# Halves of a partition's rows outermost in the tiles of q, k and v

## The chip, the cores and the metric

The kernel runs on one core of one Trainium2 chip. A core has five engines with queues of their own: PE (TensorE, matmuls, with PEld as the loading of its weights), DVE (VectorE), ACT (ScalarE), POOL (GpSimd) and SP (SyncE, which issues transfers here). Sixteen DMA engines move data. The metric is device microseconds of an execution, as a median over runs.

## The reference

Four batches, eight heads, 768 rows, head size 64, eight blocks of 96 rows. A Sinkhorn matrix P (8x8 for each head) mixes the blocks of k and of v; each block of q then attends to the mixed block at its own place; the result goes through a token-mixing layer.

```python
for _ in range(5):
    P = P - np.max(P, axis=-1, keepdims=True)
    P = np.exp(P)
    P = P / (np.sum(P, axis=-1, keepdims=True) + 1e-09)
    P = P / (np.sum(P, axis=-2, keepdims=True) + 1e-09)
k_sorted = np.einsum('bhij,bhjcd->bhicd', P, k_b).reshape(B, H, S, D)
v_sorted = np.einsum('bhij,bhjcd->bhicd', P, v_b).reshape(B, H, S, D)
scores = scale * np.matmul(q_b, k_sb.transpose(0, 1, 2, 4, 3))
...
attn_out = np.matmul(attn, v_sb).reshape(B, H, S, D)
...
wq, wk = x @ w_q, x @ w_k
W_tok = scale * np.einsum('bsd,btd->bst', wq, wk)
mixed = np.einsum('bst,btd->bsd', W_tok, x)
out = np.maximum(mixed, 0.0) @ w_out
```

## The kernel before

A batch's q, k or v (8 heads x 768 rows x 64, in f32) is loaded by one transfer that casts to bf16. Row 6p + r of a head lies in partition p at place r, so 128 partitions hold 6 rows of each head; a block of 96 rows is 16 partitions. The tiles Qn, Kn and Vn (three buffers each, NIN) are [128, head, 6 rows, 64]. `u_l` (L238 to L241) issues a load on POOL's queue: n = 0, 1, 2 is q, k, v. In DRAM a run of 6 rows of one head is contiguous, so a load is 128 x 8 pieces of 384 elements.

The work is cut into small units, each a letter with a batch, a number and an engine or a bank of PSUM. The list `ORDER` at the top of the file is their order, written out by hand; a unit is issued on its engine when the list comes to it, and waits there by semaphores for the data it reads and the buffers it writes. Each engine runs its own units in that order and never overtakes. `l` loads, `n` builds M (the Sinkhorn weights spread to a 128x128 matrix for each head; L231 to L236, on POOL or DVE), `Q` transposes q with the identity (L255), `K` sorts and transposes k with M (L264 to L277), `S` computes scores, `e` their exponential, `P` the attention output, `x` divides by the row sums; `T`, `J`, `W`, `G`, `H` and `O` are the layer behind, `y` the stores. Lower-case letters are mostly the copies out of PSUM. All matmuls go through the helper `mm` (L148), all copies through `copy` (L151), so the profile shows them as L149, L153 and L155 and they are told apart by their tiles.

v takes two ways. For batches 0 and 1 (`TURN`) it is sorted and transposed like k and then turned back by transposes (`F`). For batches 2 and 3 `V` (L282 to L289) sorts without a transpose: for each pair of rows n (2n and 2n + 1) eight matmuls with M as weights and 128 columns of Vn (two rows of a head) as the moving side; `v` (L291) copies the pair of all heads into Vs, and `R` (L298) moves one row of Vs to VT with a transfer on SP's queue.

The first entries of ORDER for POOL are the loads of k, v and q of batch 0, then q of batch 1, and further loads between the products for M. The queue works them off in the order k0, v0, q0, q1, k1, v1, k2, q2, the two halves of wqk, v2, q3, k3, v3, wo. Ahead of the sorting, TensorE runs 40 matmuls of zeros (`Z`) while the Sinkhorn steps run on DVE and ACT. At the end of the program stands a test of the row sums and a slower way behind an `If`, which these inputs don't take; the diff touches its loads too.

Of the kernel before, what the change touches and what calls it, by code (L numbers as in the profile page):

```python
# [56 lines left out]
def kernel(  # L57
# [11 lines left out]
    nc = tc.nc  # L69
    B, H, S, D = q.shape  # L70
# [3 lines left out]
    P = 128  # L74
    R6 = S // P
    SP = BLK // R6
    NP = H // 2
    D1 = D + 1
    DM = moe_w_out.shape[0]
# [18 lines left out]
    def tiles(name, n, shape, dtype=BF16):  # L98
        return [sb.tile(shape, dtype, name=f"{name}{i}") for i in range(n)]

    PS = psp.tile([P, 8, 512], FP32, name="ps")
    ENG = {"A": nc.scalar, "D": nc.vector, "P": nc.gpsimd, "S": nc.sync}
# [2 lines left out]
    nc.sync.dma_start(out=Pm[:, 0:NB, :], in_=sort_net.rearrange("b h i j -> (b h) i j"))  # L105

    NIN = 3
    Qn, Kn, Vn = (tiles(n, NIN, [P, H, R6, D]) for n in ("Qn", "Kn", "Vn"))
    wqk = sb.tile([P, PT, 2, DH], BF16, name="wqk")
    wo = sb.tile([P, PT, DM], BF16, name="wo")  # L110
    QT = tiles("QT", 2, [P, NP, R6, P])
# [1 line left out]
    Vs = tiles("Vs", 2, [P, R6, H, D1])  # L113
    VT = tiles("VT", 2, [BLK, NB, H * D1])
# [9 lines left out]
    ot = tiles("ot", NOT, [P, 2, DM], FP32)  # L124
    M = tiles("M", 2, [P, H, SP, NB])
    RS = sb.tile([BLK, B, NG, 2, AG // 2], FP32, name="RS")
# [3 lines left out]
    PbT = sb.tile([BH, 2, BH], BF16, name="PbT")  # L130
    Lx = sb.tile([BH, 4, NB, SP], BF16, name="Lx")
    tmp = sb.tile([BH, NB], FP32, name="tmp")
    idb = sb.tile([P, P], BF16, name="idb")
# [14 lines left out]
    def mm(o, w, x, start=True, stop=True, t=False):  # L148
        nc.tensor.matmul(o, w, x, is_transpose=t, start=start, stop=stop, skip_group_check=True)  # L149

    def copy(e, o, i):  # L151
        if e == "A":
            nc.scalar.copy(o, i)  # L153
        else:
            nc.vector.tensor_copy(o, i)  # L155

    def bf(n):
        return PS[:, n, :].bitcast(BF16)
# [76 lines left out]
            in1=m_p.unsqueeze(1).unsqueeze(3).to_broadcast([P, 2, SP, NB]), op=ALU.mult)  # L235


    def u_l(b, n, e):  # L238
        t, src = (Qn, Kn, Vn)[n], (q, k, v)[n]
        nc.gpsimd.dma_start(out=t[b % NIN].rearrange("p h r d -> p h (r d)"),  # L240
                            in_=src[b].rearrange("h (p r) d -> p h (r d)", p=P))  # L241

    def u_m(b, n, e):
        if n < 2:
# [10 lines left out]
    def u_Q(b, n, bank):  # L255
        ps = bf(bank)[:, 0:S].rearrange("p (r s) -> p r s", r=R6)
        for r in range(R6):
            for hh in range(2):
                mm(ps[hh * D:(hh + 1) * D, r, :], Qn[b % NIN][:, 2 * n + hh, r, :], idb, t=True)

    def u_q(b, n, e, bank):
        copy(e, QT[b % 2][:, n].rearrange("p r s -> p (r s)"), bf(bank)[:, 0:S])
# [1 line left out]
    def sorted_t(t, b, n, bank):  # L264
        ps = flat(bank)
        for r in range(R6):
            for hh in range(2):
                h = 2 * n + hh
                mm(ps[hh * D:(hh + 1) * D, r * P:(r + 1) * P], t[b % NIN][:, h, r, :],
                   M[b % 2][:, h].rearrange("p s i -> p (s i)"))  # L270

    def by_block(e, o, bank):
# [9 lines left out]
    def u_V(b, n, bank):  # L282
        if b in TURN:
            sorted_t(Vn, b, n, bank)
            return
        ps = flat(bank)
        for h in range(H):
            mm(ps[:, h * P:(h + 1) * P], M[b % 2][:, h].rearrange("p s i -> p (s i)"),
               Vn[b % NIN][:, h, 2 * n:2 * n + 2, :].rearrange("p r d -> p (r d)"))  # L289

    def u_v(b, n, e, bank):  # L291
        if b in TURN:
            by_block(e, XT[b % 2][:, n, :], bank)
            return
        copy(e, Vs[b % 2][:, 2 * n:2 * n + 2, :, 0:D].rearrange("p r h d -> p h r d"),
             flat(bank).rearrange("p (h r d) -> p h r d", h=H, r=2))

    def u_R(b, n, e):  # L298
        ENG[e].dma_start(out=VT[b % 2].rearrange("(s r) i x -> r s i x", r=R6)[n],
                         in_=Vs[b % 2][:, n].rearrange("p h e -> p (h e)"))  # L300

    def u_F(b, n, bank):
        for i in range(NB):
# [7 lines left out]
    def u_N(b, n, e):  # L311
        t = dict(q=QT, k=KT, v=Vs, f=VT, e=E, x=X)[e][b % 2]
        if e == "q":
            src = t[0:1, n, R6 - 1, P - 1:P]
        elif e == "k":
            src = t[0:1, n, S - 1:S]
        elif e == "v":
            src = t[0:1, 2 * n + 1, H - 1, D - 1:D]
        elif e == "f":
            src = t[0:1, NB - 1, (2 * n + 1) * D1:(2 * n + 1) * D1 + 1]  # L320
        elif e == "e":
            src = t[0:1, n, 0:1]
        else:
            src = t.rearrange("p k i m -> p (k i m)")[0:1, grp(n)[0] * D:grp(n)[0] * D + 1]
        nc.gpsimd.tensor_copy(gate, src)
# [125 lines left out]
    for item in ORDER.split():  # L451
        kind, b, n, arg = UNIT.match(item).groups()
        b, half = int(b), halves.get(n[-1], ())
# [22 lines left out]
    with tc.If(redo > 0, preferred_fallthrough_block=False):  # L476
        qc = QT[1].rearrange("p k r s -> p k (r s)")
        sx = XT[1][0:BLK].rearrange("p t c -> p (t c)").bitcast(FP32)[:, 0:S]
        ex = E[1][:, 1, 0:S]
        exT = E[1][:, 2, 0:S]  # L480
        mx = RS.rearrange("p b n a t -> p (b n a t)")[:, 0:NB]
        sm = RS.rearrange("p b n a t -> p (b n a t)")[:, NB:2 * NB]

        def bb(t, w):
            return t.unsqueeze(2).to_broadcast([BLK, NB, w])

        spread(0, H, BH)
        u_u(0, 1, "D", 0)
        for b in range(B):
            for n in range(3):  # L490
                nc.gpsimd.dma_start(out=(Qn, Kn, Vn)[n][0].rearrange("p h r d -> p h (r d)"),
                                    in_=(q, k, v)[n][b].rearrange("h (p r) d -> p h (r d)", p=P))
            if b == 0:
                spread(1, 0, H)
                src = PS[:, 1, 0:NB * H].rearrange("p (i h) -> p h i", h=H)
            else:
                src = PTR.rearrange("p i h -> p h i")[:, (b - 1) * H:b * H, :]
            for n in range(NP):
                spread_m("D", 0, n, src)
            for n in range(NP):  # L500
                u_Q(0, n, 2)
                u_q(0, n, "D", 2)
                copy("D", qc[:, n].rearrange("p (i r s) -> p r i s", i=NB, r=R6),
                     QT[0][:, n].rearrange("p r (i s) -> p r i s", i=NB))
                u_K(0, n, 4)
                u_k(0, n, "D", 4)
                sorted_t(Vn, 0, n, 6)
                by_block("D", XT[0][:, n, :], 6)
                u_F(0, n, 3)
                u_f(0, n, "D", 3)  # L510
            for h in range(H):
                kp, o = h // 2, h % 2 * D
                sp = PS[0:BLK, 4:6, 0:4 * BLK].rearrange("p a (i c) -> p a i c", c=BLK)
                for i in range(NB):
                    mm(sp[:, i // 4, i % 4, :], qc[o:o + D, kp, i * BLK:(i + 1) * BLK],
                       KT[0][o:o + D, kp, i * BLK:(i + 1) * BLK])
                copy("D", sx.rearrange("p (a n) -> p a n", a=2), PS[0:BLK, 4:6, 0:4 * BLK])
                s3 = sx.rearrange("p (i c) -> p i c", i=NB)
                nc.vector.reduce_max(mx, s3, axis=AX.X)
                nc.vector.tensor_sub(s3, s3, bb(mx, BLK))  # L520
                nc.scalar.activation(ex, sx, ACT.Exp, scale=scale)
                nc.vector.reduce_sum(sm, ex.rearrange("p (i c) -> p i c", i=NB), axis=AX.X)
                nc.vector.reciprocal(sm, sm)
                for i in range(NB):
                    mm(bf(6)[0:BLK, i * BLK:(i + 1) * BLK], ex[:, i * BLK:(i + 1) * BLK],
                       idb[0:BLK, 0:BLK], t=True)
                copy("D", exT, bf(6)[0:BLK, 0:S])
                op = PS[0:BLK, 7, :].rearrange("p (i d) -> p i d", d=D)
                for i in range(NB):
                    mm(op[:, i, :], exT[:, i * BLK:(i + 1) * BLK], VT[0][:, i, h * D1:h * D1 + D])  # L530
                nc.vector.tensor_mul(X[0][:, kp, :, o:o + D], op, bb(sm, D))
            for n in range(PT):
                u_T(0, n, n % 2)
                u_t(0, n, "D", n % 2)
            for n in range(2):
                u_J(0, n, 2)
                u_j(0, n, "D", 2)
                u_d(0, n, "D")
                u_W(0, n, 3)
                u_w(0, n, "D", 3)  # L540
            for n in range(2):
                u_G(0, n, 2)
            u_g(0, 0, "D", 2)
            for n in range(3):
                u_H(0, n, 4)
                u_h(0, n, "D", 4)
            for n in range(R6):
                u_O(0, n, n % 2)
                u_o(b, n, "D", n % 2)
                if b == LAST or n % 2:  # L550
                    u_y(b, n if b == LAST else n // 2, "P")
# [30 lines left out]
```

## Time and profile before

| | us |
|---|---|
| median of 3 runs | 108.27 (107.89 to 108.35) |
| the profiled execution, its own time | 108.6 |
| its span, first to last instruction | 106.8 |
| TensorE busy | 94.2 (88%) |
| DVE busy | 74.1 (69%) |
| ACT busy | 69.9 (65%) |
| POOL busy | 31.3 (29%) |

| transfer, by the page's part 6 | times | KB each | median us, issue to landing |
|---|---|---|---|
| Kn from k | 4 | 768 | 12.8 |
| Vn from v | 4 | 768 | 14.7 |
| Qn from q | 4 | 768 | 15.1 |
| wo | 1 | 512 | 22.7 |
| wqk, each of two | 1 | 64 | 14.3, 14.7 |
| VT from Vs | 12 | 130 | 2.5 |

The KB are those written. A busy share is over the whole span; the span has stages with different limits, and the page's rows of 40 slices (2.67 us each) show where. "Landing" counts from the issue, so it holds the time that a load stands in the queue behind others. Granted TensorE clock: 0.981 in the mean; it falls only in the last slices, where TensorE has no work.

### The profile page before, as it was taken

How to read it: one execution, taken by the hardware profiler on the slowest of the kernel's cores; microseconds unless marked ns; L12 is line 12 of the kernel's file. 1: busy time of each engine (PE TensorE's matmuls, PEld its weight loads, DVE VectorE, ACT ScalarE, POOL GpSimd, SP SyncE). 2: the span in 40 equal slices, each digit the busy share in tenths (PEclk: the TensorE clock that was granted, in tenths of full speed). 3: DMA queues.
4: the chain of work that ended last, by engine and by line, in shares of the span. 5: the costliest groups of instructions: out<-in, count | busy, mean ns of one | idle time of the engine just before them, and what ended most of it. 6: DMA issues, size and time to landing. Idle time of an engine off the chain costs nothing.

```text
span 106.8 us, 3637 instructions
## 1 busy us (share of the span) xinstructions
PE 94.2 (88%) x1556; PEld 65.7 (61%) x1556; DVE 74.1 (69%) x144; ACT 69.9 (65%) x101; POOL 31.3 (29%) x51
## 2 busy tenths in 40 slices
PE   5999989597698979889999999999999999999600
PEld 2334489486686966779868867597666565454300
DVE  2687689198797785788989977999767765455200
ACT  4101079769687879898879798688933448784400
POOL 5999089999229400000000000000077000000000
PEclk9999999999999999999999999999999999999975
DMA  0899999999999999999975373100059145496950
GB/s 3 91 201 205 203 203 210 200 203 205 205 204 204 188 202 211 198 203 208 205 161 159 94 211 96 44 6 0 6 196 388 45 196 203 160 408 236 381 196 18
DMA packets 18501, 18.57 MB, mean 174 GB/s; under 512 B 1840, under 2 KB 16560, under 8 KB 18480
## 3 DMA queue, kind: packets, MB, share of 16 engines
q0 software_dynamic: 14064, 10.09, 62.8%
q1 hardware_dynamic: 4416, 8.19, 22.0%
q8 instruction: 14, 0.23, 0.9%
q14 instruction: 7, 0.06, 0.1%
HBM read 20.19 MB, written 6.29 MB: 248 GB/s over the span
## 4 chain that ended last, share of the span: by engine, by line
PE 80%; ACT 6%; issue 4%; DVE 3%; DVEq 0%; ACTq 0%
PE ps L149 80%; ACT E L339 3%; DVE X L364 1%; ACT Vs L153 1%; DVE KT L155 1%; ACT XT L153 1%; ACT QT L153 1%; ACT ot L153 1%; DVE M L233 0%; DVE wk L155 0%; DVE fil L170 0%; DVE RS L362 0%; DVE Pm L169 0%; DVEq L155 0%; ACTq L153 0%
## 5 line engine op out<-in xcount | busy, mean ns | idle before, releaser
L339 ACT ACTIVATE E<-ps 96x960 bf16<-96x960 f32 (+1 forms) x28 | 24.6, 905 | 2.9 <-PE ps L149 2.6
L149 PE MATMUL ps<-wo,mixT 128*128 128x512 bf16 (+1 forms) x100 | 22.9, 371 | 0.0
L364 DVE TENSOR_TENSOR X<-ps,RS 96x896 bf16<-96x896 f32 (+1 forms) x20 | 20.1, 1007 | 0.7
L149 PEld LDWEIGHTS <-mixT 128*128 128x128 bf16 x100 | 8.9, 98 | 8.6 <-issue 0.2
L153 ACT COPY ot<-ps 128x512 f32<-128x512 f32 (+1 forms) x16 | 8.8, 560 | 8.1 <-PE ps L149 4.7
L468 POOL TENSOR_SCALAR ok<-RS 96x280 bf16<-96x280 f32 x1 | 0.9, 924 | 41.9 <-DVE RS L362 41.9
L149 PE MATMUL ps<-fil 128*128 128x512 bf16 x40 | 11.7, 466 | 1.2 <-DVE fil L170 1.2
L149 PE MATMUL ps<-VT,E 96*128 96x65 bf16 x256 | 11.2, 194 | 1.4 <-DVE X L364 0.8
L149 PEld LDWEIGHTS <-E 96*128 96x128 bf16 x256 | 9.8, 97 | 3.6 <-issue 1.5
L149 PE MATMUL ps<-QT,KT 64*128 64x96 bf16 x256 | 9.9, 204 | 1.6 <-issue 1.3
L233 POOL TENSOR_TENSOR M<-PTR,m_p 128x256 bf16<-128x256 bf16 x12 | 8.8, 750 | 7.4 <-PE ps L149 4.1
L155 DVE COPY ot<-ps 128x512 f32<-128x512 f32 x9 | 6.1, 691 | 6.1 <-PE ps L149 3.2
L149 PEld LDWEIGHTS <-fil 128*128 128x128 bf16 x40 | 4.5, 116 | 7.9 <-issue 3.8
L153 ACT CAST KT<-ps 128x768 bf16<-128x768 f32 x10 | 7.7, 805 | 2.0 <-PE ps L149 1.9
L149 PEld LDWEIGHTS <-KT 64*128 64x128 bf16 x256 | 6.8, 94 | 2.9 <-issue 1.6
L149 PE MATMUL ps<-idb,X 96*128 96x96 bf16 x128 | 7.5, 206 | 0.6 <-issue 0.6
L149 PE MATMUL ps<-M,Kn 128*64 128x128 bf16 x192 | 7.5, 221 | 0.3 <-issue 0.3
L155 DVE COPY QT<-ps 128x768 bf16<-128x768 bf16 x13 | 6.7, 551 | 1.4 <-PE ps L149 1.1
L425 ACT ACTIVATE mixT<-ps 128x1024 bf16<-128x1024 f32 x7 | 7.0, 1026 | 0.9 <-PE ps L149 0.6
L149 PEld LDWEIGHTS <-X 96*128 96x128 bf16 x128 | 6.2, 98 | 1.9 <-issue 0.9
L155 DVE COPY VT<-ps 96x1024 bf16<-96x1024 bf16 x7 | 4.8, 687 | 3.5 <-PE ps L149 2.7
L149 PE MATMUL ps<-idb,Qn 128*64 128x128 bf16 x192 | 7.0, 220 | 0.1
(78 smaller groups left out, 154.0 us busy)
## 6 DMA issues: line engine op xcount, KB each, us to landing
out_dram<-ot SPq DMA_DIRECT2D x9, 512.0 KB, 2.8
Kn<-in_k_dram POOLq DMA_DIRECT2D x4, 768.0 KB, 12.8
Vn<-in_v_dram POOLq DMA_DIRECT2D x4, 768.0 KB, 14.7
Qn<-in_q_dram POOLq DMA_DIRECT2D x4, 768.0 KB, 15.1
VT<-Vs SPq DMA_DIRECT2D x12, 130.0 KB, 2.5
out_dram<-ot SPq DMA_DIRECT2D x6, 256.0 KB, 2.7
wo<-in_moe_w_out_dram POOLq DMA_DIRECT2D x1, 512.0 KB, 22.7
qD<-qkT SPq DMA_DIRECT2D x6, 48.0 KB, 2.6
```

The costliest lines, as they stand in the source:

```text
L149: nc.tensor.matmul(o, w, x, is_transpose=t, start=start, stop=stop, skip_group_check=True)
L153: nc.scalar.copy(o, i)
L155: nc.vector.tensor_copy(o, i)
L233: ENG[e].tensor_tensor(out=M[b % 2][:, h0:h1], in0=src[:, h0:h1].unsqueeze(2).to_broadcast([P, 2, SP, NB]), in1=m_p.unsqueeze(1).unsqueeze ...
L339: nc.scalar.activation(E[b % 2][:, n, 0:2 * w * BLK].rearrange("p (t a c) -> p a t c", a=2, c=BLK), PS[0:BLK, bank:bank + 2, 0:w * BLK].re ...
L364: nc.vector.tensor_mul(xo.rearrange("p (a t d) -> p a t d", a=2, d=D), ps[:, :, :, 0:D], rs.unsqueeze(3).to_broadcast([BLK, 2, w, D]))
L425: nc.scalar.activation(o, i, ACT.Relu)
L468: nc.gpsimd.tensor_scalar(out=okf, in0=rsf, scalar1=1e-30, scalar2=None, op0=ALU.is_ge)
```

## The change

The tiles of q, k and v become [128, half, head, 3 rows, 64]: row r of a head is now at half r // 3, place r % 3. A load's pieces are 3 rows (192 elements), 128 x 16 of them. Readers of single rows go through the new helper `row`. In V's sorting for batches 2 and 3, a pair of rows must be one access with a fixed step: pairs are now (0,1), (3,4) and (2,5), the last of which takes two runs of 64 columns, one from each half. `v` copies to those two rows of Vs, and `R`, which is called in the same order as before, moves the row that belongs to its number.

```diff
+    R3 = R6 // 2
+    ROWS = ((0, 1), (3, 4), (2, 5))
...
-    Qn, Kn, Vn = (tiles(n, NIN, [P, H, R6, D]) for n in ("Qn", "Kn", "Vn"))
+    Qn, Kn, Vn = (tiles(n, NIN, [P, 2, H, R3, D]) for n in ("Qn", "Kn", "Vn"))
...
+    def load(t, src):
+        nc.gpsimd.dma_start(out=t.rearrange("p c h r d -> p c h (r d)"),
+                            in_=src.rearrange("h (p c r) d -> p c h (r d)", p=P, c=2))
+
+    def row(t, b, h, r):
+        return t[b % NIN][:, r // R3, h, r % R3, :]
+
     def u_l(b, n, e):
         t, src = (Qn, Kn, Vn)[n], (q, k, v)[n]
-        nc.gpsimd.dma_start(out=t[b % NIN].rearrange("p h r d -> p h (r d)"),
-                            in_=src[b].rearrange("h (p r) d -> p h (r d)", p=P))
+        load(t[b % NIN], src[b])
...
-                mm(ps[hh * D:(hh + 1) * D, r, :], Qn[b % NIN][:, 2 * n + hh, r, :], idb, t=True)
+                mm(ps[hh * D:(hh + 1) * D, r, :], row(Qn, b, 2 * n + hh, r), idb, t=True)
...
-                mm(ps[hh * D:(hh + 1) * D, r * P:(r + 1) * P], t[b % NIN][:, h, r, :],
+                mm(ps[hh * D:(hh + 1) * D, r * P:(r + 1) * P], row(t, b, h, r),
                    M[b % 2][:, h].rearrange("p s i -> p (s i)"))
...
             mm(ps[:, h * P:(h + 1) * P], M[b % 2][:, h].rearrange("p s i -> p (s i)"),
-               Vn[b % NIN][:, h, 2 * n:2 * n + 2, :].rearrange("p r d -> p (r d)"))
+               Vn[b % NIN][:, 0:2, h, 2, :] if n == 2 else Vn[b % NIN][:, n, h, 0:2, :])
...
-        copy(e, Vs[b % 2][:, 2 * n:2 * n + 2, :, 0:D].rearrange("p r h d -> p h r d"),
+        r0, r1 = ROWS[n]
+        copy(e, Vs[b % 2][:, r0:r1 + 1:r1 - r0, :, 0:D].rearrange("p r h d -> p h r d"),
              flat(bank).rearrange("p (h r d) -> p h r d", h=H, r=2))

     def u_R(b, n, e):
-        ENG[e].dma_start(out=VT[b % 2].rearrange("(s r) i x -> r s i x", r=R6)[n],
-                         in_=Vs[b % 2][:, n].rearrange("p h e -> p (h e)"))
+        r = ROWS[n // 2][n % 2]
+        ENG[e].dma_start(out=VT[b % 2].rearrange("(s r) i x -> r s i x", r=R6)[r],
+                         in_=Vs[b % 2][:, r].rearrange("p h e -> p (h e)"))
```

The loads on the slower way behind the `If` go through `load` as well. A line of `u_N`, a unit that ORDER does not use, follows the new pairs.

More of the change, by code (lines that the diff above doesn't have):

```diff
@@ L317, in u_N @@
         elif e == "v":
-            src = t[0:1, 2 * n + 1, H - 1, D - 1:D]
+            src = t[0:1, ROWS[n][1], H - 1, D - 1:D]
         elif e == "f":
@@ L490 @@
             for n in range(3):
-                nc.gpsimd.dma_start(out=(Qn, Kn, Vn)[n][0].rearrange("p h r d -> p h (r d)"),
-                                    in_=(q, k, v)[n][b].rearrange("h (p r) d -> p h (r d)", p=P))
+                load((Qn, Kn, Vn)[n][0], (q, k, v)[n][b])
             if b == 0:
```

## The prediction

> **What bounds the kernel now.** I read the page's parts 2, 3 and 4 first, then the waits of TensorE, its timeline, the answers by tile, and the windows.
>
> ```profile
> PE 80%; ACT 6%; issue 4%; DVE 3%; DVEq 0%; ACTq 0%
> ```
>
> This is the chain of waits, by engine: TensorE is 80% of it, and no DMA appears. So everything that stops TensorE before about 100 us is paid in full. The transfers bind in a quieter way:
>
> ```profile
> PEclk9999999999999999999999999999999999999975
> DMA  0899999999999999999975373100059145496950
> q0 software_dynamic: 14064, 10.09, 62.8%
> q8 instruction: 14, 0.23, 0.9%
> ```
>
> The clock is granted in full while TensorE works. From slice 2 to slice 20 (about 4 to 54 us) the 16 DMA engines never rest; queue 0, on which POOL issues the loads, is what fills them. Queue 8 carries 14 packets of instructions. They matter here:
>
> ```profile
> PE ps L149 <- issue: 3.2, 5, 1.3
> ...
> 20.54 0.20 PE L149 MATMUL ps<-QT,KT 64*128 64x96 bf16 x1 [1.29 <-issue]
> ...
> 26.46 0.38 PE L149 MATMUL ps<-VT,E 96*128 96x65 bf16 x7 [0.58 <-issue]
> ...
> 32.49 0.58 PE L149 MATMUL ps<-M,Vn 128*64 128x128 bf16 x13 [0.40 <-issue]
> ...
> 38.96 0.39 PE L149 MATMUL ps<-idb,X 96*128 96x96 bf16 x5 [0.56 <-issue]
> ...
> 44.98 0.36 PE L149 MATMUL ps<-M,Kn 128*64 128x128 bf16 x6 [0.32 <-issue]
> ```
>
> Five stops, 3.15 us together, with no releaser. Counting TensorE's weight loads and matmuls in order of start, they stand ahead of numbers 449, 705, 961, 1217 and 1473: every 256 instructions, about 6.0 us apart. The packet records of queue 8 hold one 16,384-byte packet ahead of each (starts 18.22, 24.24, 30.21, 36.62, 42.65, each 0.95 long), and TensorE goes on 1.3 to 1.5 us after the packet's end. So TensorE runs out of code. A block is evidently asked for when the one before it is entered: from there to the packet's start it takes 3.1, 3.6, 3.7, 4.1, 3.6, 3.7 us while loads run, and 0.5, 0.9, 0.4 us once they have ended (mean 0.6). About 3.0 us of each fetch is spent behind loads.
>
> A sentence on the skill: the Trainium skill ("Runtime: NRT & Kernel Launch", Instruction fetch mechanics) says that code comes in blocks of 16 KiB, 256 instructions, and that crossing one is mostly hidden; the 256 agrees with this trace, the hiding does not, and by that rule the stops would be worth nothing to change.
>
> **The price of a load.** Each load is 1024 packets of 768 bytes written (1536 read, the cast halves them), 64 per engine. The completion packets of an engine lie 3860 ns apart from load to load: 60.3 ns per packet. The neighbours on the same queue are wqk (128 bytes written, 256 read; 32 per engine in 434 ns, 13.6 ns each) and wo (1024 written, 2048 read; 32 in 2543 ns, 79.5 ns).
>
> ```profile
> 20.00:24.00 4.00, 3.46 (x81) 2.96 (x80) 2.50 (x5) 2.58 (x4) 3.97 (x7) 1.00 1.32 204
> ...
> 35.00:36.00 1.00, 1.00 (x25) 0.82 (x21) 0.30 (x2) 0.71 (x1) 0.96 (x2) 1.00 1.96 170
> ```
>
> The last column is GB/s: 204 in loads, 170 where wqk's small packets are mixed in.
>
> **Part by part.** The two programs hold the same instructions in the same order on each engine; only the twelve loads differ, 128x16x192 elements in place of 128x8x384.
>
> *Twice the packets.* After the change: 2048 packets of 384 bytes written, 768 read. On the straight line between 256 (13.6) and 1536 (60.3) this is 13.6 + 512/1280 x 46.7 = 32.3 ns; twice is 64.6 in place of 60.3, +7%, +0.27 us a load. The line from 1536 to 2048 leaves 2.7 ns fixed: at least 64 x 2.7 = +0.17 us. The far end is the packets' own recorded length (32 ns, 79 ns, 98 ns for the three kinds): 51 ns at 384 bytes, twice is 102 against 79, +29%, +1.12 us. I take 0.25, since gaps between completions measure throughput and the recorded lengths overlap (the busy share of 1.31 says so).
>
> Two sentences on the skill: "DMA: Bandwidth & Descriptors" (Specifications) asks for at least 512 B per transfer and names a read-modify-write below it, which speaks against this change, though wqk's 128-byte writes show no such price here. Its "Why small descriptors are slow" gives 3 cycles per packet, by which I estimate 31.8 ns and +0.23 us a load; if a load's time doubled under 512 B, I estimate +3.9 us a load and a kernel tens of us slower.
>
> *Issuing.* POOL takes 0.89 to 0.98 us (means) for a load's 1024 packets and 0.75 to 0.82 for the 512 of wqk or wo, so 2048 cost about 1.2, bounds 0.9 (nothing) and 1.9 (in proportion).
>
> ```profile
> L240 POOL DMA_DIRECT2D Kn<-in_k_dram x4: 893/939/1129, 1.3 to 26.4; - x4
> ...
> L246 POOL DMA_DIRECT2D wqk<-in_moe_w_q_dram x1: 815/815/815, 22.3 to 22.3; - x1
> ```
>
> Only the first is exposed: everything on the queue starts 0 to 0.9 us later, I take 0.3. The later ones are issued while four loads lie ahead in the queue, which hides them; uncovered, each would cost its 0.3. POOL's products for M (L233) queue behind them and come up to 2 us later by 27 us; batch 1 reads its last M at about 29, and n3.0 waits for TensorE at 31.4 anyway. wo is issued after K of batch 2 has landed (32.4, later 34.9) and not read until 63.
>
> *Landing against first use* (completion records; first TensorE instruction that reads the tile): Q0 16.11/16.77, Q1 20.73/22.02, K1 24.59/26.78, V1 28.45/30.73, Q2 36.25/40.23, V2 41.11/45.27, Q3 44.97/50.99, V3 52.69/56.11. With 0.3 + 0.25 per load: Q0 17.2 (0.4 late), Q1 22.0 (just in time), K1 26.1, V1 30.3, V3 56.0 (just in time). Q0's 0.4 vanishes in the stop at 19.3, which ends when the code comes. So slower loads alone cost nothing as long as the stops remain.
>
> *The fetch.* How is its 3.0 us counted? On the engine that carries them (its completions come late by 1.1 us), the six packets of queue 8 start 41, 16, 48, 8, 48 and 16 packets into a load, all but the first in steps of 8, and mostly some 60 packets after the request. The fetch from 32.49 has wqk in its way: 46 packets of a load, 64 small ones, 8 of the next load, 118 in all, yet it took 4.1 us. So the wait goes by bytes or time, and not by number. It then stretches with the loads by 7%: 3.0 x 0.07 = +0.21, with the packet's own time and its tail about +0.23 per fetch. Bounds: 0.15, and 0.4 if all 6.0 us stretch. Six blocks (up to number 1729) are bound like this: 6 x 0.23 = 1.4, less the 0.2 that the sixth had to spare, +1.2 us. V3 at 56.0 is then covered, being read at 57.3. Behind that TensorE has no pause in which it could win this back.
>
> *V by pairs.* One of three groups of 8 matmuls reads its moving 128 columns as two runs of 64, batches 2 and 3 only. QT is read by L149 in six runs of 16 at 203 ns against 219 for 128 contiguous columns: nothing. Were their pitch (24 such matmuls in 1.72 us, 72 ns) doubled, 16 of them would cost +1.2. The evictions into Vs keep their shape (1.03 us on ACT), and the twelve row transfers keep size and order: nothing.
>
> **Sum.** 106.8 span + 1.2 = 108.0; with the 1.8 that this execution (108.6) has around its span, 109.8; it lies 0.33 over the median 108.27. So 109.5, own range 108.8 to 110.5.
>
> **Rivals.** *The stops go* (chance 0.35): the wait is counted in packets after all, and halves (3.0 to 1.6), so the 3.15 us of stops vanish. For it: the quanta of 8 packets. Against: the fetch beside wqk. The new bound is then data: Q1 comes at 22.0, where it was read before, V3 at 56.0, where it was read at 56.1, and all of TensorE's work after V3 follows. Time 108.27 - 0.1, about 108.1; with the load's low price (V3 at 52.69 + 12 x 0.17 + 0.3 = 55.0) 107.2, with 0.28 and 0.9 of issue 109.1. This is the side that is not slower: it gains as soon as a load costs less than +0.26 us beside the 0.3 of issue. *The loads slow by 29%* (0.10): V3 lands at 52.69 + 13.4 + 0.3 = 66.4, 10.3 late: about 118.6. It decides from +0.35 us a load on, where V3 passes the 57.3 of my forecast. *Neither moves* (0.05): the price of a packet is hidden, 108.3.
>
> **Chances.** My forecast has 0.50. About 0.5%, 0.54 us, is what a measurement can tell from no change: 107.7 to 108.8. Faster: half of the first rival, 0.18. Same: 0.13 of that rival, 0.05 of my case, 0.04 of the last: 0.22. Slower: 0.45 of my case, 0.04 of the first rival, 0.10 and 0.01: 0.60. The range 107.3 to 110.8 holds my case and nearly all of the first rival; the slow loads stay outside.
>
> **What would show it.** GB/s in the loaded slices near 190 instead of 204 (158 if the rival of slow loads is right); loads that issue in 1.2 us; TensorE's stops without releaser still there every 256 instructions, 6.2 us apart, five or six of them. If they are gone and the wait ahead of V's matmuls of batch 3 appears in their place, the first rival is right. I am wrong if the stops shrink while the loads keep their pace.

## The result, and the profile after

| | before | after |
|---|---|---|
| median, us | 108.21 (107.89 to 108.35, 4 runs) | 109.71 (109.45 to 109.79, 4 runs) |
| ratio, 95% interval | | 1.0137 [1.0114, 1.0161] |
| profiled execution, its own time and span | 108.6, 106.8 | 109.73, 107.8 |

The changed kernel is 1.4% slower, 1.5 us; 109.5 was forecast.

The page of the changed kernel, its clock, DMA share, GB/s and queues:

```profile
PEclk9999999999958999999999999999999999999995
DMA  0699999999999999999999374200039245296960
GB/s 3 63 191 192 192 193 196 189 193 194 192 195 191 190 183 192 195 192 194 194 205 248 106 204 117 70 6 0 0 141 383 105 195 201 112 409 257 366 224 17
...
q0 software_dynamic: 26352, 10.09, 78.4%
q8 instruction: 14, 0.23, 0.8%
```

Queue 0 moves the same 10.09 MB in 26,352 packets where it needed 14,064. The loaded slices show 189 to 196 GB/s and once 183 (forecast 190; 198 to 211 and once 188 before), and reach one to two slices further. The two low digits of the clock are 3.4 us at half clock (29.5 to 32.9 us), which only some profiles have; the third experiment comes to the same end without them.

The answers by tile and by window: loads as POOL issues them, and the stretch of 20 to 24 us (last three columns: clock, DMA share, GB/s):

```profile
L241 POOL DMA_DIRECT2D Kn<-in_k_dram x4: 1262/1378/1582, 1.3 to 28.1; - x4
...
20.00:24.00 4.00, 3.71 (x101) 3.11 (x96) 2.40 (x5) 3.41 (x6) 4.00 (x6) 1.00 1.60 192
```

The completions of a DMA engine now lie 4.086 us apart (3.860 before): 31.9 ns per packet, +0.226 us a load.

TensorE's waits and its timeline in the changed kernel:

```profile
PE ps L151 <- issue: 2.1, 5, 0.9
PE ps L151 <- DMA Vn<-in_v_dram: 1.4, 1, 1.4
...
PE ps L151 <- DMA Qn<-in_q_dram: 0.7, 1, 0.7
```

```profile
18.05 0.86 PE L151 MATMUL ps<-idb,Qn 128*64 128x128 bf16 x24 [0.71 <-DMA Qn<-in_q_dram]
...
20.82 0.20 PE L151 MATMUL ps<-QT,KT 64*128 64x96 bf16 x1 [0.29 <-issue]
...
27.02 0.38 PE L151 MATMUL ps<-VT,E 96*128 96x65 bf16 x7 [0.86 <-issue]
...
45.81 0.36 PE L151 MATMUL ps<-M,Kn 128*64 128x128 bf16 x6 [0.60 <-issue]
...
56.93 1.05 PE L151 MATMUL ps<-Vn,M 128*128 128x128 bf16 x12
58.20 0.83 PE L151 MATMUL ps<-Vn,M 128*128 128x128 bf16 x12 [0.22 <-issue]
```

The sums mislead here. The stops without releaser fell from 3.2 to 2.1 us, and 2.1 us of waits for v and q of batch 0 came up, so it looks as if late data had replaced late code. But the stop at 20.82 is short only because TensorE came late to it; it still ends when the code arrives. What counts is when each block of 256 instructions is entered (weight loads and matmuls counted in order of start; the time is the start of the matmul there):

| block entered at instruction | 193 | 449 | 705 | 961 | 1217 | 1473 | 1729 | 1985 |
|---|---|---|---|---|---|---|---|---|
| before, us | 15.09 | 20.67 | 26.50 | 32.49 | 39.02 | 45.01 | 51.19 | 57.10 |
| after, us | 15.46 | 20.95 | 27.05 | 33.77 | 39.57 | 45.84 | 52.03 | 58.31 |
| after less before | 0.37 | 0.28 | 0.55 | 1.28 | 0.55 | 0.82 | 0.85 | 1.21 |

The 0.37 of late data is gone at 449. The 1.28 at 961 holds what the half clock cost; the kernel before stops for 0.56 us ahead of 1217 and the changed one for 0.06, which takes it in again. The rest is built up at some of the blocks, and 1.20 us remain at the last matmul (101.66 against 100.45).

### The profile page after: what moved, and what is told of

Same layout as the page of the kernel before. It is cut to its first block, busy times and chain, and to the rows that moved or that the text cites. A ratio compares the mean times of both kernels' runs of the same rounds, so it can differ in the third digit from the quotient of the medians.

```text
span 107.8 us, 3630 instructions
## 1 busy us (share of the span) xinstructions
PE 94.4 (88%) x1549; PEld 66.4 (62%) x1556; DVE 74.1 (69%) x144; ACT 69.8 (65%) x101; POOL 35.3 (33%) x51
## 3 DMA queue, kind: packets, MB, share of 16 engines
q0 software_dynamic: 26352, 10.09, 78.4%
## 4 chain that ended last, share of the span: by engine, by line
PE 66%; DMA 13%; DVE 5%; issue 5%; POOL 3%; ACT 3%; DVEq 0%; POOLq 0%; ACTq 0%
PE ps L151 66%; DMA Qn<-in_q_dram 13%; DVE VT L157 2%; DVE X L374 2%; POOL Kn L241 1%; ACT Vs L155 1%; POOL Vn L241 1%; DVE KT L157 1%; ACT E L349 1%; ACT ot L155 1%; DVE XT L157 1%; DVE RS L372 0%; POOL idb L191 0%; POOL idb L190 0%; ACT XT L155 0%
## 5 line engine op out<-in xcount | busy, mean ns | idle before, releaser
L151 PE MATMUL ps<-wo,mixT 128*128 128x512 bf16 (+1 forms) x93 | 22.2, 370 | 0.5 <-issue 0.2
L151 PE MATMUL ps<-VT,E 96*128 96x65 bf16 x256 | 11.7, 198 | 1.7 <-issue 0.9
L151 PEld LDWEIGHTS <-E 96*128 96x128 bf16 x256 | 10.3, 100 | 4.0 <-issue 1.7
L151 PE MATMUL ps<-fil 128*128 128x512 bf16 x40 | 11.0, 443 | 1.2 <-DVE fil L172 1.2
L151 PE MATMUL ps<-M,Kn 128*64 128x128 bf16 x192 | 8.0, 227 | 0.7 <-issue 0.6
L372 DVE RECIPROCAL RS<-ps 96x14 f32<-96x14 f32 (+1 forms) x20 | 4.6, 228 | 3.9 <-PE ps L151 3.9
L151 PEld LDWEIGHTS <-Kn 128*64 128x64 bf16 x192 | 6.3, 113 | 1.5 <-issue 0.7
```

The source lines that it names most:

```text
L372: nc.vector.reciprocal(rs, ps[:, :, :, D])
```

## The experiments

All ratios are to the kernel before in the same set of runs, on the same chip.

**The pairs of V alone.** Loads as before; the pairs (0,1), (3,4), (2,5) read two runs of 64 columns from a tile of 6 rows.

```diff
+    ROWS = ((0, 1), (3, 4), (2, 5))
...
-               Vn[b % NIN][:, h, 2 * n:2 * n + 2, :].rearrange("p r d -> p (r d)"))
+               Vn[b % NIN][:, h, ROWS[n][0]:ROWS[n][1] + 1:ROWS[n][1] - ROWS[n][0], :])
...
+        r = ROWS[n // 2][n % 2]
```

> The kernel before with V of batches 2 and 3 sorted by the row pairs (0,1), (3,4), (2,5); loads as before. Theory (all of the loss comes through the loads and what queues behind them): 108.2 us, ratio 1.000 within 0.003. Rival (reading two runs of 64 columns, or the rows of Vs at a step of 3, costs something): up to 109.7.

108.34 us, ratio 1.0017 [0.9998, 1.0037]. The pairs are at most 0.4 us of the loss, and the interval allows for none.

**Batch 0's loads alone, and the other nine alone.** A table gives the number of outermost parts for each batch; tiles and readers follow it.

```diff
+    CUT = (2, 1, 1, 1)
...
+        if CUT[b] == 1:
+            nc.gpsimd.dma_start(out=cut(t, b)[:, 0].rearrange("p h r d -> p h (r d)"),
+                                in_=src.rearrange("h (p r) d -> p h (r d)", p=P))
+        else:
+            nc.gpsimd.dma_start(out=cut(t, b).rearrange("p c h r d -> p c h (r d)"),
+                                in_=src.rearrange("h (p c r) d -> p c h (r d)", p=P, c=CUT[b]))
```

> Only batch 0's three loads in pieces of 3 rows; the other nine as before. Theory: v of batch 0 lands about 1.4 us later, as in the changed kernel, and is read 0.4 us later; the code fetches behind the later loads keep their 3.6 us. +0.4 us, 108.6. Rival (the lateness of the last loads is what counts, 3.8 us of it for +1.2 us of TensorE): all later loads are 1.6 us late, +0.5. Rival (all of the loss is in the start): +1.2 to +1.5.

108.67 us, ratio 1.0018 [0.9993, 1.0042]: nothing that is clear of noise. In its trace TensorE is 1.97 us late ahead of the first stop (half clock from 14.2 to 17.6 us included) and 0.53 behind it.

The other nine: `CUT = (1, 2, 2, 2)`.

> Batch 0's three loads as before, the other nine in pieces of 3 rows, with V by the new pairs in batches 2 and 3. Theory: no delay of batch 0, code fetches 0.15 us longer each while loads run, and the fetch at the end of the loads waits for them longer: +0.5 to +0.9 us, 108.7 to 109.1. Rival (all of the loss is in the start): 108.2. Rival (the stops do not matter, only landing does): v of batch 3 lands at 54.7 and is read at 56.1, so 108.2.

109.70 us, ratio 1.0108 [1.0078, 1.0137]: most of the loss, and by TensorE's last matmul all of it, with batch 0 as before. The timeline of TensorE in this kernel, its stops and the first matmuls on v of batch 3:

```profile
20.82 0.20 PE L151 MATMUL ps<-QT,KT 64*128 64x96 bf16 x1 [1.47 <-issue]
...
27.02 0.38 PE L151 MATMUL ps<-VT,E 96*128 96x65 bf16 x7 [0.86 <-issue]
...
33.32 0.58 PE L151 MATMUL ps<-M,Vn 128*64 128x128 bf16 x13 [0.68 <-issue]
...
39.79 0.39 PE L151 MATMUL ps<-idb,X 96*128 96x96 bf16 x5 [0.56 <-issue]
...
46.09 0.36 PE L151 MATMUL ps<-M,Kn 128*64 128x128 bf16 x6 [0.60 <-issue]
...
57.21 1.82 PE L151 MATMUL ps<-Vn,M 128*128 128x128 bf16 x24
```

They are the five stops of before at the same work, 1.29, 0.58, 0.40, 0.56 and 0.32 us there, 4.17 together in place of 3.15. Held against the kernel before, instruction by instruction from the first matmul on v, TensorE's delay starts at 0.10 us and changes nowhere by more than 0.15 us at once except at four block boundaries: +0.18 at 449, +0.27 at 705, +0.28 at 961, +0.27 at 1473; 0.11 more comes at 1985. Of each of the three larger steps 0.12 to 0.19 us is a longer wait of the code packet, and most of the rest lies between its end and TensorE's going on. Its last matmul ends at 101.67, as in the changed kernel. Meanwhile v of batch 3 landed at 54.75, 2.1 us later than before, and was read at 57.21 without a wait: the late landing took nothing. The rival that only landing counts has fallen, and so has the one that all is in the start.

**A later start in the old pieces.** Two memsets on POOL ahead of the first load.

```diff
+        if (b, n) == (0, 1):
+            nc.gpsimd.memset(RS, 1.0)
+            nc.gpsimd.memset(Lx, 0.0)
```

> The kernel before with two memsets on POOL (about 1.2 us) ahead of the first load, so that all loads start 1.2 us later in their old pieces. Theory: only batch 0's v matters, it lands at 13.5 in place of 12.25 and is read about 0.2 us later: 108.2 to 108.5. Rival (every late landing is paid): +1.2 us, 109.4.

108.57 us, ratio 1.0015 [0.9990, 1.0041]. The dose failed: POOL had idled there, and the first load's issue only moved from 1.29 to 1.49 us, its landing by 0.3. This run says nothing on lateness.

**Other block boundaries.** More and shorter filler matmuls for the same time.

```diff
-        for _ in range(n):
-            mm(PS[:, bank, :], fil[:, 0:P], fil)
+        for _ in range(96):
+            mm(PS[:, bank, 0:P], fil[:, 0:P], fil[:, 0:P])
+        for _ in range(16):
+            mm(PS[:, bank, :], fil[:, 0:P], fil)
```

> The kernel before with 112 filler matmuls in place of 40 (96 of 128 columns, then 16 of 512: as many columns, 144 instructions more). If TensorE's stops are fetches of code in blocks of 256 instructions, all of them move to other work but stay at instruction numbers 449 + 256 k, and the fetch that made the first stop is asked for in the filler, some 5 us earlier: the first stop (1.3 us) goes and later ones come earlier: -1.0 to -1.6 us, 106.6 to 107.2. Rival (the stops belong to the work at which they stand, or to late data): they stay at that work, 108.2.

109.21 us, ratio 1.0079 [1.0057, 1.0102]. The timeline of TensorE, its longer stops:

```profile
23.17 0.38 PE L149 MATMUL ps<-idb,Qn 128*64 128x128 bf16 x7 [1.04 <-issue]
...
29.25 0.20 PE L149 MATMUL ps<-VT,E 96*128 96x65 bf16 x1 [0.30 <-issue]
...
35.18 0.26 PE L149 MATMUL ps<-QT,KT 64*128 64x96 bf16 x3 [0.63 <-issue]
...
53.31 0.35 PE L149 MATMUL ps<-QT,KT 64*128 64x96 bf16 x8 [0.52 <-issue]
```

The stops moved to other work and stand ahead of instructions 705, 961, 1217 and 1985, again a multiple of 256 from 449, where there is now none. That settles what they are: code that is not there yet. The time went the other way than I expected. Held against the kernel before at the same work, TensorE moves between 1.1 us ahead and 0.5 behind, as the stops stand elsewhere, and is 0.36 ahead when it comes to the last stop. That one stands ahead of 1985, at work where the kernel before has none, and leaves TensorE 0.34 us behind. Another 0.33 us comes at 64.5 us, at no block boundary: a row transfer into VT lands at 64.43 (63.42 before), and the matmuls on VT start at 64.52 (63.86). The 0.67 us then stay to the last matmul. Why that transfer lands later is open.

> The changed kernel with the same filler. Theory: the stops shrink as in the kernel before, but v of batch 3 lands at 56.5 and was read at 56.9, so a wait for it takes their place: 109.3 to 109.7, with a wait for Vn ahead of its matmuls at 57. Rival (late data is no bound of the changed kernel): 108.1 to 108.7.

111.30 us, ratio 1.0254 [1.0199, 1.0308], 1.2% above the changed kernel's own ratio of 1.0137. Both expectations missed. Stops of 0.93, 0.58, 0.90 and 0.68 us stand at 705, 961, 1217 and 1985, and at 67.0 us TensorE stands for a row transfer into VT that landed at 66.90; the changed kernel enters that work without a stop. So the loss sits in part at the same two places as in the run before. v of batch 3 landed at 56.4 and was read at 58.6. Whether its landing would bound the changed kernel without the stops is left open by this.

**Still smaller pieces.** `CUT = (3, 3, 3, 3)`: 3072 packets a load of 256 bytes written.

> All loads in pieces of 2 rows (three outermost parts, pairs of V as before). By the line through the packets of 256, 768 and 1536 bytes read, 22.4 ns a packet, 4.3 us a load. If a code fetch waits for a number of packets (60), it starts about 2.0 us after it is asked for; if for bytes or time, 3.8 to 4.2 us. In both cases v of batch 3 lands near 60 us and is what TensorE waits for: about 113 us.

113.38 us in a single run (108.33 before). A load took 4.31 us, as expected, and v of batch 3 landed at 58.7 and was waited for. TensorE's timeline, two stops and that wait:

```profile
34.10 0.58 PE L151 MATMUL ps<-M,Vn 128*64 128x128 bf16 x13 [0.87 <-issue]
...
46.74 0.36 PE L151 MATMUL ps<-M,Kn 128*64 128x128 bf16 x6 [0.74 <-issue]
...
59.07 1.51 PE L151 MATMUL ps<-Vn,M 128*128 128x128 bf16 x24 [1.12 <-DMA Vn<-in_v_dram]
```

How long a code fetch waits, from the entry of the block before (us, by the packet records of queue 8), in five kernels:

| asked for at instruction | 449 | 705 | 961 | 1217 | 1473 |
|---|---|---|---|---|---|
| 6 rows a piece (before) | 3.6 | 3.7 | 4.1 | 3.6 | 3.7 |
| 3 rows, all (changed) | 3.7 | 3.9 | 3.4 | 3.8 | 3.8 |
| 3 rows, batches 1 to 3 | 3.7 | 3.9 | 4.1 | 3.8 | 3.9 |
| 2 rows, all | 3.9 | 4.1 | 4.0 | 3.9 | 4.0 |
| 6 rows, paced by half loads (below) | 1.3 | 1.4 | 1.8 | 0.7 | 0.2 |

Three times as many packets, each a third, and the wait is 3.85 to 4.08 where I had expected some 2.0 from a count of packets (60 of them, at 22.4 ns, are 1.3 us). It does not go by the number of packets.

**Fewer loads posted at a time.** Loads from k of batch 1 on are cut by heads, and each part is issued when the one two (three) before it has landed; M of batch 1 is built ahead of them.

```diff
+        first = (b, n) in ((0, 1), (0, 2), (0, 0), (1, 0))
+        w = H if first else H // 2
+        for h in range(0, H, w):
+            if not first:
+                nc.gpsimd.tensor_copy(gate, posted[-2])
+            nc.gpsimd.dma_start(out=t[b % NIN][:, h:h + w].rearrange("p h r d -> p h (r d)"),
+                                in_=src[b][h:h + w].rearrange("h (p r) d -> p h (r d)", p=P))
+            posted.append(t[b % NIN][0:1, h, 0, 0:1])
```

> The kernel before, its loads from k of batch 1 on cut by heads into two transfers, each issued only when the last but one has landed, so that an engine never has more than some 64 packets of loads posted, 30 to 60 ahead of a code fetch. If a fetch waits for what is posted on its engine, it starts 2 to 3.6 us after it is asked for (3.1 to 4.1 before), and the stops shrink by up to 1.5 us together; the price is gaps between loads where POOL issues late, up to the 3.4 us that v of batch 3 has to spare: 106.8 to 108.3. If the fetch's wait is the price of a busy memory and not of what is posted, waits and stops stay: 108.2 to 108.8.

> The same with four transfers a load, each issued when the third before it has landed: at most 48 packets posted. If a fetch waits for what is posted: 1.5 to 3 us, stops shrink further; POOL issues 32 transfers of about 0.7 us between 16 and 50 us and may leave gaps between them: 106.5 to 109. If not: waits as before, 108.2 to 109.5.

124.05 us, ratio 1.1452 [1.1392, 1.1513], and 130.62 us, 1.2078 [1.2021, 1.2135]. POOL and the windows of the kernel with halves:

```profile
21.38 0.18 POOL L246 COPY gate<-Qn 1x1 bf16<-1x1 bf16 x1 [3.87 <-DMA Qn<-in_q_dram]
21.82 0.74 POOL L247 DMA_DIRECT2D Kn<-in_k_dram  x1 [0.27 <-DVE VT L155]
```

```profile
20.00:24.00 4.00, 3.71 (x91) 3.18 (x90) 2.76 (x6) 2.69 (x4) 2.06 (x5) 1.00 0.79 103
...
28.00:32.00 4.00, 2.31 (x64) 1.79 (x61) 3.08 (x5) 3.08 (x4) 0.92 (x3) 1.00 0.91 128
```

The code came early, as the table's last row shows, and behind the first stop (1.18 us) none of over 0.1 us is left, so a fetch does wait for what is posted ahead of it. But the engines ran dry (103 and 128 GB/s), so data came late; one wait of TensorE for q takes 3.6 us. Most of its waiting is for M (7.3 us with halves, 13.1 with quarters), which POOL builds in turn with its issues, and these now stand still until a landing. TensorE's clock was also granted at half for 13.7 us between 32 and 73 us; how much of the loss that is was not separated. The part issued at 21.82 waited for a landing at 20.92 and landed on its first engine at 25.84; less the 1.93 us of its own transfer, the first of its packets moved some 3.0 us after that landing. Of these, 0.9 pass until POOL's issue begins, 0.7 in it, and 1.3 to 1.4 behind it.

> As e8_paced_halves, but each half load is issued when the third before it has landed: 64 to 96 packets of loads posted on an engine instead of 32 to 64. From landing to the first packet of the next transfer took 3.0 us there, about 50 packets, so here the engines should mostly stay fed. Theory (a fetch waits for what is posted, up to some 60 packets): waits of 3.0 to 3.7 us and stops as in the kernel before, time 108 to 111, depending on the gaps that are left; the depth that keeps the engines fed is the depth that a fetch waits for. Rival (a little pacing gives short waits and full loads at once): waits under 2.5 us and 106 to 107.5.

113.06, 115.06, 115.42 and 116.89 us in 4 runs, without an interval, at granted clocks of 0.94 to 0.96; the profile is of the longest. There the fetches waited 2.9, 4.8, 2.5, 0.0 and 1.4 us, and the loads moved 191 GB/s from 20 to 24 us but 150 from 28 to 32. It doesn't tell the two expectations apart, but no version here beats the kernel before.

## Why the prediction was right

- *What bounds the kernel.* Right: stops at blocks of 256 instructions. The moved boundaries show it, and the paced loads show that the loads are what the code waits behind.
- *The price of a load.* 0.25 us taken, 0.226 measured, inside its bounds; the far end of 29% is out. The 3 cycles per packet that the Trainium skill gives ("DMA: Bandwidth & Descriptors", Why small descriptors are slow) had led to an estimate of +0.23, which these runs bear out. The read-modify-write under 512 B that its Specifications name does not show as a loss at 384 or at 256 bytes written (31.9 and 22.4 ns per packet).
- *Issuing.* A load's issue takes 1.25 to 1.38 us in the median (1.2 forecast). Its effect on the first load was mis-sized: all 16 engines have ended k of batch 0 at 9.55 in place of 8.39, 0.93 more than its longer transfer explains, and I took 0.3 (upper bound 0.9). So v of batch 0 was read 0.37 late, which I had at nothing, and q 1.28 late instead of 0.4. It cost nothing in the end, by the cover that the prediction named: the first stop took it in.
- *Landing against first use.* v of batch 3 landed at 56.5 (56.0 forecast) and was read at 56.9 (57.3). It was covered, but hardly: the semaphore of the landing, which comes a little behind the last packet, is at 56.85, 0.08 us ahead of the read.
- *The fetch.* +0.23 us was forecast for each of six blocks, less 0.2, together 1.2. With batch 0 as before it was +0.18 to 0.28 at four of them and nothing at 1217 and 1729, 1.1 us by 1473 with the 0.10 from ahead of them; the changed kernel has 0.85 by 1729, and 0.36 more at 1985, where the fetch waited 3.7 us (2.7 before), the loads now ending later. The cause is the one forecast, but that the total fits so well is partly luck: there are fewer blocks that pay, most of them pay a little more, and 1985 was held to be free.
- *V by pairs.* Forecast at nothing; 1.0017 [0.9998, 1.0037].
- *Sum.* 1.2 us of span forecast, 1.0 measured (1.2 at TensorE's last matmul), and 109.71 against 109.5 in the median.
- *Rivals.* That the stops go by a count of packets is out, by the thirds. The slow loads are out by 4.086 us a load, and "neither moves" by that and the ratio of 1.0137.

## What to carry to other kernels

Sort an engine's idle time without releaser by instruction number before looking for data: stops at a fixed distance of instructions point to missing code, and a change of the transfers can then act through the queue that the code stands in, even where every tile lands in time. A sum of waits can shift from one name to another without anything having moved; compare when the same instruction is reached in both kernels. Twice the packets in a queue that never rests can be a price at each fetch behind it, and needs a gain somewhere to be worth it.

## What the runs showed that I had not expected

- A code fetch stands behind about 60 packets of 1536 bytes read on its engine, or behind as many bytes in smaller packets: 3.6 to 4.1 us, against 0.2 to 1.8 us where few loads were posted. The Trainium skill ("DMA: Bandwidth & Descriptors", Queues, rings and completion order) describes an engine that alternates between queues after each packet of at most 64 descriptors. A wait of some 60 of the trace's packets lies near that ceiling, but the wait was nearly the same in time for 64 packets a load as for 192, which a limit by count does not explain. What sets the depth stays open.
- It matters at which work a block of code ends. 72 additional short filler matmuls (144 instructions), with the filler no longer than before (11.5 against 11.7 us), moved the stops and made the kernel 0.8% slower, with less time in stops without a releaser (2.8 against 3.2 us).
- Between a landing that POOL waits for and the first packet of the transfer that it then issues lie about 3.0 us, three quarters of a whole load's 3.9.
